# An attention kernel with a maxout behind it: output stores issued by ScalarE, and batch sums of v taken by halves of the heads

## The chip, the cores and the metric

The kernel runs on one core of a Trainium2 chip. A core has five engines that work beside each other, each through its own list of instructions in a fixed order: TensorE (PE) for matmuls, VectorE (DVE), ScalarE (ACT) and GpSimd (POOL) for elementwise work, and SyncE (SP), which here only issues transfers (DMAs). Engines wait for each other through semaphores. The metric is the time of one execution in microseconds (us) on the device, as a median of several runs.

## The reference

The inputs are q, k and v of 4 batches, 8 heads, 768 positions and 64 features, and three weight matrices. Cut to what matters:

```python
k_sum = k.reshape(B, H, nb, block, D).max(axis=3)       # block = 32, nb = 24
v_sum = v.reshape(B, H, nb, block, D).mean(axis=3)
scores_l = scale * np.matmul(q, k.transpose(0, 1, 3, 2)) # kept where |i - j| < 16
scores_s = scale * np.einsum('bhsd,bhnd->bhsn', q, k_sum) + np.log(block)
a = softmax(np.concatenate([masked scores_l, scores_s], axis=-1))
attn = np.matmul(a, np.concatenate([v, v_sum], axis=2))
x = attn.transpose(0, 2, 1, 3).reshape(B * S, H * D)    # 3072 x 512
g = np.maximum(x @ w1, x @ w2)                           # 3072 x 1024
out = g @ w_out                                          # 3072 x 512, float32
```

Each position attends to its near neighbours and to 24 block summaries, the largest k and the mean v of each block of 32. The attention's output goes through a maxout and a last matrix.

## The kernel before, in words

The work is written as a list of operations, each with an engine, an estimated time, what it reads and writes, and a priority. A planner (`Plan`, L112 to L188) goes through time in steps of 0.02 us and gives each engine the first operation in order of priority whose inputs are ready and whose buffers are free. What comes out is a fixed order of instructions per engine; the planner's times have no further part in the execution. `bump` in `CFG` shifts the priority of single operations.

For each batch and pair of heads, k and q are loaded (L361, L366), cast to bf16 and turned so that features lie on partitions: by PE (L509) or, for some pairs of the later batches, by transposing DMAs that SP issues (L471, L476). The scores of 64 positions at a time are matmuls with 64 rows of contraction (L566), ACT takes the exponential (L591), DVE masks (L598), and PE multiplies with v (`values`, L614), whose 64 x 65 blocks are written in pairs to the upper and the lower 64 rows. DVE divides by the sum (L627), and the result is turned by PE or by a DMA (L632) into `xt`.

The v side is `cast_v` and `spread_v`. A tile `vx` holds for each 64 positions a 128-row operand: rows of v, and in 32 of its rows the block means, the same for every one of the six 128-position groups. `spread_v` copies the odd groups (L407), lets PE sum the blocks with a matrix `amean` (L421), evicts the sums from PSUM to a tile `sums` (L434) and copies that into the rows of `vx` that want it (L438 to L443). For batch 0 this runs per pair of heads, for batches 1 to 3 once for all eight heads. For batches 1 and 2 the last copies are DVE's, for batch 3 they are two DMAs issued by SP (L448).

The maxout works on 256 positions at a time: four matmul groups with w1 − w2 (L723) with a ReLU on ACT behind each (L728), and then for each half of 128 positions the output (`out_part`): matmuls with w2's product (L744) and with g (L751), a copy from PSUM to a tile `o` (L754, four such tiles in turn), mostly by ACT, and a store to DRAM (L762). Rows are shifted by 16 positions, so that the last block of a batch wraps and needs a second, short store (L764). The very last block is cut into three column parts; the store of its first part is issued by ACT, those of the others, copied by DVE, by SP. All other stores are issued by SP, in SP's fixed order among loads and transposing DMAs.

The helper `copy` (L451) records a copy on DVE, ACT or POOL, so most copies have the line L456 in the profile.

The program was built for both kernels, and each DMA in it signals its landing on one of eight semaphores, taken in turn in the order of the program; before a DMA is issued, its engine waits until the DMA that used the same semaphore eight places earlier has landed.

Of the kernel before, what the change touches and what calls it, by code (L numbers as in the profile page):

```python
# [16 lines left out]
ACT = mybir.ActivationFunctionType  # L17

CFG = dict(
    kd="....D..DD.DD", xd="D...DD.DD.DDDDDDDD", tus=(1.6, 1.0, 1.2), kc="ADDA", qc="APPP", kp="DADD", qp="DDDA",
    tl="AADA", od="DADP", se="DADA", sr="DPdP", vc="ADPA", sc=4, s0=4, ph=1, ph0=2, av=4, lkp="DDDA", lxt="DADAAD",
    idle=40, pz=1, wd="PPDD", w1b="DPFD", w1t="AAAA", wo="PAAD", xt="DDDDDA", kv=(0.2, 1.2, 4.2, 4.2), sp=0.7,
# [56 lines left out]
class Task:  # L81
    done, start = 1e9, None
# [29 lines left out]
class Plan:  # L112
# [9 lines left out]
    def op(self, engine, us, fn, read=(), write=(), change=(), touch=(), behind=(), prio=0.0, label="", port=False):  # L122
        t = Task()
        t.engine, t.us, t.fn, t.label = engine, us, fn, label
        t.port = engine == "POOL" or port and engine == "DVE"
        t.prio = (prio + CFG["bump"].get(label, 0), len(self.tasks))
        t.new, t.behind = [*write, *change], behind
        t.deps = {w for b in (*read, *change) for w in b.writers}
        for b in t.new:
            b.writers.append(t)  # L130
        for b in (*read, *touch, *t.new):
            b.users.append(t)
        self.tasks.append(t)
        return t
# [57 lines left out]
def kernel(  # L192
# [14 lines left out]
    nc = tc.nc  # L207
    B, H, S, D = 4, 8, 768, 64
# [6 lines left out]
    NM, J, VW = S // 128, S // 128, 66  # L215
# [3 lines left out]
    op = plan.op  # L219
# [157 lines left out]
    def by_parity(b):  # L377
        return vx[b].ap[:].rearrange("p (m w) h c -> p w m h c", w=2)
# [12 lines left out]
    def spread_v(b, h0, h1, prio, engines):  # L391

        n, hs = h1 - h0, slice(h0, h1)
        src = [mains[b, hp] for hp in range(h0 // 2, h1 // 2)]
        out = [vx[b], *(ready[b, hp] for hp in range(h0 // 2, h1 // 2))]
        took, ps, st = Buf(Ring([None])), Buf(banks, "mm"), Buf(stg)
        tag, whole = f"{b}{h0}", n == H
        s_rows = slice(96, 128)
        if whole:
            fresh = Buf(Ring([None]))  # L400
            op("POOL", 0.2, lambda: nc.gpsimd.memset(by_parity(b)[s_rows, 0, :, :, D:VW], 1.0),
               read=[mains[b, 0]], write=[vx[b], fresh], prio=prio, label=f"ones {b}")
            src = [*src, fresh]

        def odd(lo, hi, ms, shift):
            w, ds = by_parity(b), slice(0, VW if whole else D)
            return (w[lo:hi, 1, ms, hs, ds],  # L407
                    w[lo:hi, 0, slice((ms.start + shift) % NM, (ms.stop + shift - 1) % NM + 1), hs, ds])

        for i, (lo, hi, ms, shift) in enumerate((  # L410
                (64, 128, slice(0, NM), 0), (0, 32, slice(0, NM - 1), 1), (0, 32, slice(NM - 1, NM), 1))):
            cols = (ms.stop - ms.start) * n * D
            move(engines[0], {"D": 0.12 + cols * 0.0003, "P": 0.06 + cols * 0.00095, "A": 0.2 + cols * 0.00083,
                              "S": (2.0, 0.83, 0.2)[i]},
                 lambda lo=lo, hi=hi, ms=ms, shift=shift: odd(lo, hi, ms, shift),
                 read=src, write=[*out, took], prio=prio, label=f"odd v{tag}{i}")

        def sums():
            w = by_parity(b)
            for m in range(NM):  # L420
                nc.tensor.matmul(out=bank(ps, n * D), lhsT=amean[:, m, :], rhs=w[:, 0, m, hs, 0:D],  # L421
                                 start=(m == 0), stop=(m == NM - 1))
# [22 lines left out]
    def move(engine, us, aps, label, **kw):  # L445
        if engine != "S":
            return copy(engine, us, aps, label, **kw)
        op("SP", us["S"], lambda: (lambda o, i: nc.sync.dma_start(  # L448
            out=o.rearrange("p m h c -> p m (h c)"), in_=i.rearrange("p m h c -> p m (h c)")))(*aps()), label=label, **kw)

    def copy(engine, us, aps, label, port=True, **kw):  # L451
        engine = ENG[engine]
        us = us if isinstance(us, float) else us[engine[0]]
        def fn():
            o, i = aps()
            {"DVE": nc.vector.tensor_copy, "ACT": nc.scalar.copy,  # L456
             "POOL": nc.gpsimd.tensor_copy}[engine](out=o, in_=i)
        op(engine, us, fn, label=label, port=port, **kw)

    def on(e):  # L460
# [277 lines left out]
    def out_part(b, grp, u, x, g, o, c0, c1, prio, engine, on_act):  # L738
        ps, cols, part = Buf(banks, "mm"), slice(c0, c1), (c1 - c0) / 512
        sl, done = slice(128 * u, 128 * u + 128), Buf(Ring([None]))  # L740

        def first():
            for c in range(KC):
                nc.tensor.matmul(out=bank(ps, c1 - c0), lhsT=x.ap[:, c, sl], rhs=w1o[c].ap[:, cols],  # L744
                                 start=(c == 0), stop=False)

        op("PE", 0.87 * part, first, read=[x, *w1o], write=[ps], prio=prio + 1, label=f"out {b}{grp}{u}")
        for n in range(2):
            def more(n=n):
                for f in range(4 * n, 4 * n + 4):  # L750
                    nc.tensor.matmul(out=bank(ps, c1 - c0), lhsT=g.ap[:, f, sl],  # L751
                                     rhs=wo[f // 2].ap[:, f % 2, cols], start=False, stop=(f == FC - 1))
            op("PE", 0.87 * part, more, read=[g, *wo], change=[ps], prio=prio + 1, label=f"out {b}{grp}{u}")
        copy(engine, {"A": 0.18 + 0.42 * part, "D": 0.15 + 0.55 * part}, lambda: (  # L754
            o.ap[:, cols], bank(ps, c1 - c0)),
             read=[ps], write=[o, done], prio=-1, port=False, label=f"copy out {b}{grp}{u}")

        def store():
            at = grp * GT + u * 128 + 16
            n = min(128, S - at)  # L760
            queue = nc.scalar if on_act else nc.sync
            queue.dma_start(out=out[b * S + at:b * S + at + n, cols], in_=o.ap[0:n, cols])  # L762
            if n < 128:
                queue.dma_start(out=out[b * S:b * S + 128 - n, cols], in_=o.ap[n:128, cols])  # L764
# [92 lines left out]
```

## Time and profile before

| | |
|---|---|
| median of 3 runs | 173.17 us (172.45 to 174.05) |
| the profiled execution | 174.17 us, its span 172.5 us |
| PE busy | 160.5 us |
| DVE busy | 102.4 us |
| ACT busy | 93.9 us |
| POOL busy | 41.7 us |
| moved by DMA | 35.82 MB, mean 208 GB/s |
| granted TensorE clock | 1.0 throughout |

The page of the profile shows one execution: the busy time of each engine, the span in 40 slices with the busy share of each in tenths, the DMA queues, the chain of work that ended last (followed back from the last instruction, at each step to what released it), and the costliest groups of instructions. A name such as `ACT o L456` is an instruction of ACT at line 456 that writes tile `o`; `SPq` is an instruction of SP's queue that issues a DMA, and its duration includes what it waits for while it issues. The trace behind the page answers in rows of a timeline: start and duration in us, engine, line, operation, out<-in, count, and in brackets the idle time before it with what ended it. Instructions that are not an engine's own work, such as the issue of a DMA, are not counted as busy.

### The profile page before, as it was taken

What the parts mean: (1) busy time and instruction counts of PE and PEld (TensorE: products, weight loads), DVE (VectorE), ACT (ScalarE), POOL (GpSimd) and SP (SyncE); (2) the same over time, 40 slices, a digit from 0 to 9 for tenths busy, and PEclk for the clock granted to TensorE, in tenths of its full rate; (3) what the DMA queues carried; (4) which work ended last, traced back from release to release, by engine and by line L of the source; (5) the groups of instructions that cost most, each with busy time, mean ns of one, the idle gap of its engine ahead of it and who ended that gap; (6) DMA issues with size and microseconds to landing.
All of it is one profiled execution on the core that took longest, in us unless ns stands there. A gap on an engine that the chain in (4) does not pass through costs nothing.

```text
span 172.5 us, 4501 instructions
## 1 busy us (share of the span) xinstructions
PE 160.5 (93%) x1841; PEld 106.6 (62%) x1841; DVE 102.4 (59%) x220; ACT 93.9 (54%) x146; POOL 41.7 (24%) x73
## 2 busy tenths in 40 slices
PE   4785898999999999999999999999998899999992
PEld 4765566997564565585574665745746658756662
DVE  6788998997679995649946466636364560000001
ACT  3766873789752658172284583852763706524420
POOL 7715899042134250053101101100400100000000
PEclk9999999999999999999999999999999999999999
DMA  5999999999999999996597999795588726011113
GB/s 169 307 321 279 313 392 379 301 288 350 297 291 192 289 335 276 174 144 183 105 209 158 345 233 215 153 241 122 99 207 132 206 51 182 2 61 65 61 61 122
DMA packets 68980, 35.82 MB, mean 208 GB/s; under 512 B 56544, under 2 KB 62944, under 8 KB 68960
## 3 DMA queue, kind: packets, MB, share of 16 engines
q1 hardware_dynamic: 68816, 35.41, 82.8%
q8 instruction: 14, 0.23, 0.6%
q10 hardware_dynamic: 144, 0.13, 0.2%
q14 instruction: 6, 0.05, 0.1%
HBM read 25.17 MB, written 6.29 MB: 182 GB/s over the span
## 4 chain that ended last, share of the span: by engine, by line
PE 63%; DMA 17%; SPq 14%; DVE 2%; issue 1%; ACT 1%; POOL 0%; DVEq 0%
PE banks L723 20%; PE banks L751 19%; PE banks L744 8%; DMA wf<-in_moe_w_dram 6%; SPq L366 5%; PE banks L707 4%; PE banks L614 4%; DMA kqf<-in_q_dram 4%; DMA vf<-in_v_dram 3%; SPq L372 3%; PE banks L509 2%; PE banks L566 2%; DMA vx<-sums 2%; SPq L659 2%; PE banks L421 2%
## 5 line engine op out<-in xcount | busy, mean ns | idle before, releaser
L751 PE MATMUL banks<-wo,g 128*128 128x512 bf16 (+2 forms) x208 | 46.9, 363 | 0.0
L723 PE MATMUL banks<-xt,wd 128*128 128x256 bf16 x384 | 46.5, 273 | 0.0
L723 PEld LDWEIGHTS <-wd 128*128 128x128 bf16 x384 | 36.8, 98 | 6.6
L728 ACT ACTIVATE g<-banks 128x512 bf16<-128x512 f32 x48 | 28.6, 598 | 15.6 <-PE banks L723 15.5
L456 ACT COPY o<-banks 128x512 f32<-128x512 f32 (+1 forms) x24 | 13.8, 576 | 35.3 <-PE banks L751 21.2
L751 PEld LDWEIGHTS <-g 128*128 128x128 bf16 x208 | 18.5, 98 | 17.8
L744 PE MATMUL banks<-w1o,xt 128*128 128x512 bf16 (+2 forms) x104 | 23.7, 363 | 0.0
L456 POOL CAST kqb<-kqf 128x768 bf16<-128x768 f32 x12 | 11.2, 934 | 39.2 <-PE banks L509 16.6
L591 ACT ACTIVATE pba<-banks 128x1024 bf16<-128x1024 f32 x16 | 16.4, 1023 | 5.6 <-PE banks L566 5.6
L528 DVE TENSOR_REDUCE ks<-kx 128x24 bf16<-128x768 bf16 x16 | 15.0, 946 | 6.0 <-DMA kx<-kqb 5.8
L627 DVE TENSOR_TENSOR xs<-banks,inv 128x512 bf16<-128x512 f32 x24 | 16.3, 686 | 0.6
L456 DVE COPY o<-banks 128x128 f32<-128x128 f32 x2 | 0.6, 290 | 26.8 <-PE banks L751 26.8
L744 PEld LDWEIGHTS <-xt 128*128 128x128 bf16 x104 | 9.8, 98 | 8.8
L598 DVE TENSOR_TENSOR pba<-pba,mask 128x1024 bf16<-128x1024 bf16 x12 | 8.3, 688 | 7.9 <-ACT pba L591 7.9
L456 POOL CAST vx<-vf 128x768 bf16<-128x768 f32 x7 | 6.4, 917 | 25.0 <-DMA vf<-in_v_dram 24.9
L566 PEld LDWEIGHTS <-kx 64*128 64x128 bf16 x416 | 7.4, 96 | 7.5 <-issue 6.3
L456 ACT CAST kqb<-kqf 128x768 bf16<-128x768 f32 x9 | 7.9, 881 | 6.7 <-DMA kqf<-in_q_dram 2.7
L456 DVE CAST kqb<-kqf 128x768 bf16<-128x768 f32 x11 | 6.7, 637 | 6.2 <-DMA kqf<-in_k_dram 4.4
L456 POOL COPY kx<-kx 128x32 bf16<-128x32 bf16 (+1 forms) x12 | 4.9, 405 | 22.2 <-DMA kx<-kqb 16.0
L785 PE MATMUL banks<-zeros 128*128 128x128 bf16 x80 | 8.5, 259 | 1.8 <-DVE zeros L781 1.8
L566 PE MATMUL banks<-qx,kx 64*128 64x64 bf16 (+2 forms) x416 | 9.4, 190 | 0.5 <-issue 0.5
L591 ACT ACTIVATE pbb<-banks 128x512 bf16<-128x512 f32 x16 | 9.6, 598 | 0.2 <-PE banks L566 0.2
(82 smaller groups left out, 189.7 us busy)
## 6 DMA issues: line engine op xcount, KB each, us to landing
kqf<-in_k_dram SPq DMA_DIRECT2D x16, 384.0 KB, 6.2
kqf<-in_q_dram SPq DMA_DIRECT2D x16, 384.0 KB, 5.7
vf<-in_v_dram SPq DMA_DIRECT2D x16, 384.0 KB, 6.4
out_dram<-o SPq DMA_DIRECT2D x19, 256.0 KB, 3.8
wf<-in_moe_w_dram SPq DMA_DIRECT2D x4, 1024.0 KB, 9.4
wf<-in_moe_w_out_dram SPq DMA_DIRECT2D x2, 1024.0 KB, 8.9
out_dram<-o SPq DMA_DIRECT2D x4, 224.0 KB, 2.5
vx<-sums SPq DMA_DIRECT2D x2, 198.0 KB, 3.6
```

The costliest lines, as they stand in the source:

```text
L366: op("SP", (1.2, 1.13)[n], lambda f=f, src=src: nc.sync.dma_start(out=f.ap[:], in_=src[b, 2 * hp:2 * hp + 2].rearrange("h (p j) d -> p h ( ...
L456: {"DVE": nc.vector.tensor_copy, "ACT": nc.scalar.copy, "POOL": nc.gpsimd.tensor_copy}[engine](out=o, in_=i)
L528: op("DVE", 0.95, lambda: nc.vector.tensor_reduce(out=ks.ap[:], in_=free(kt(), 128, [256, NM], [192, 2], [32, 2], [1, 32]), axis=AX.X, op= ...
L566: nc.tensor.matmul(out=bank(ps[i], 1024)[:, 512 * a + at + n0:512 * a + at + n1], lhsT=kx[b, hp].ap[r, 128 * t + 128:128 * t + 256], rhs=q ...
L591: op("ACT", (1.03, 0.6)[i], lambda: nc.scalar.activation(out=pv(), in_=bank(ps, 1024).rearrange("p (a c) -> p a c", a=2)[:, :, 0:64 * n], ...
L598: op("DVE", (0.69, 0.43)[i], lambda: nc.vector.tensor_tensor(out=pv(), in0=pv(), in1=m, op=ALU.mult), read=[mask_in], change=[pb], prio=pr ...
L627: op("DVE", 0.69, lambda: nc.vector.tensor_tensor(out=x.ap[:], in0=av()[:, :, :, 0:D], in1=inv.ap[:].to_broadcast([128, 2, 4, D]), op=ALU. ...
L723: nc.tensor.matmul(out=bank(ps)[:, 256 * s:256 * s + 256], lhsT=wd[n].ap[:, c, 128 * s:128 * s + 128], rhs=x.ap[:, c, :], start=(c == 0), ...
L728: op("ACT", 0.6, lambda n=n, ps=ps: nc.scalar.activation(out=g.ap[:, 2 * n:2 * n + 2, :].rearrange("p f n -> p (f n)"), in_=bank(ps), func ...
L744: nc.tensor.matmul(out=bank(ps, c1 - c0), lhsT=x.ap[:, c, sl], rhs=w1o[c].ap[:, cols], start=(c == 0), stop=False)
L751: nc.tensor.matmul(out=bank(ps, c1 - c0), lhsT=g.ap[:, f, sl], rhs=wo[f // 2].ap[:, f % 2, cols], start=False, stop=(f == FC - 1))
L785: nc.tensor.matmul(out=bank(ps, 128), lhsT=zeros[:], rhs=zeros[:], start=True, stop=True)
```

## The change

It has two parts.

First, where ACT copies an output block to its tile `o`, the store is no longer an operation of SP with a place in SP's order: ACT issues it itself, directly behind its copy (`copied`, with the short second store of a wrapped block). The operation `store` stays in the planner's list, but does nothing. The two stores behind DVE's copies stay with SP, and the one that ACT had issued stays with ACT. The planner sees the same operations with the same times, and so each engine's order is unchanged but for the stores themselves.

Second, the sums of v for batches 1 to 3 are taken by halves of the heads. In place of six matmuls of all 128 columns of `amean` with the 512 columns of eight heads, there are twelve in pairs: columns 0 to 63 of `amean` with heads 0 to 3 (256 columns) into PSUM rows 0 to 63, and columns 64 to 127 with heads 4 to 7 into rows 64 to 127 of the same 256 columns. Both halves of `amean` hold the same sums, so each half of the rows now has the sums of four heads. The eviction reads 256 columns instead of 512. The copies into `vx` are four of half the width instead of two, since the two groups of heads lie on different rows; for batch 3 that is four DMAs issued by SP.

```diff
+    smc="CCC",
...
+        halves = whole and CFG["smc"][b - 1] == "C"
+
         def sums():
             w = by_parity(b)
+            if halves:
+                for m in range(NM):
+                    for i in range(2):
+                        r = slice(64 * i, 64 * i + 64)
+                        nc.tensor.matmul(out=bank(ps, n * D // 2)[r], lhsT=amean[:, m, r],
+                                         rhs=w[:, 0, m, n // 2 * i:n // 2 * i + n // 2, 0:D],
+                                         start=(m == 0), stop=(m == NM - 1))
+                return
...
+        if halves:
+            sums_by_halves(b, ps, st, took, out, prio, engines)
+            return
...
+    def sums_by_halves(b, ps, st, took, out, prio, engines):
+
+        n = H // 2
+        copy(engines[1], {"D": 0.12 + H * D * 0.0011, "A": 0.18 + H * D * 0.00083}, lambda: (
+            st.ap[:, 0:n, 0:D], bank(ps, n * D).rearrange("p (h d) -> p h d", d=D)),
+             read=[ps, blocks_in], write=[st], prio=prio, port=False, label=f"sums {b}0")
+        cols = 6 * H * VW
+        for w, r in ((0, slice(96, 128)), (1, slice(32, 64))):
+            def aps(half, w=w, r=r):
+                frm = slice(32 + 64 * half, 64 + 64 * half)
+                return (by_parity(b)[r, w, :, n * half:n * half + n],
+                        st.ap[frm, 0:n].rearrange("p h d -> p (h d)").rearrange(
+                            "p (o h d) -> p o h d", o=1, d=VW).to_broadcast([32, NM, n, VW]))
+            move(engines[2], {"D": 0.12 + cols * 0.0003, "P": 0.06 + cols * 0.00095, "A": 0.2 + cols * 0.00083, "S": 1.0},
+                 aps, halves=True, read=[st, *([took] if w == 0 else [])], write=out, prio=prio, label=f"all sums {b}0{w}")
...
-        copy(engine, {"A": 0.18 + 0.42 * part, "D": 0.15 + 0.55 * part}, lambda: (
-            o.ap[:, cols], bank(ps, c1 - c0)),
-             read=[ps], write=[o, done], prio=-1, port=False, label=f"copy out {b}{grp}{u}")
-
-        def store():
+        own = engine == "A" and not on_act
+
+        def aps():
+            return o.ap[:, cols], bank(ps, c1 - c0)
+
+        def copied():
+            nc.scalar.copy(out=aps()[0], in_=aps()[1])
+            store(nc.scalar)
+
+        if own:
+            op("ACT", 0.18 + 0.42 * part, copied, read=[ps], write=[o, done], prio=-1, label=f"copy out {b}{grp}{u}")
+        else:
+            copy(engine, {"A": 0.18 + 0.42 * part, "D": 0.15 + 0.55 * part}, aps,
+                 read=[ps], write=[o, done], prio=-1, port=False, label=f"copy out {b}{grp}{u}")
+
+        def store(queue):
             at = grp * GT + u * 128 + 16
             n = min(128, S - at)
-            queue = nc.scalar if on_act else nc.sync
             queue.dma_start(out=out[b * S + at:b * S + at + n, cols], in_=o.ap[0:n, cols])
...
-        op("ACT" if on_act else "SP", 0.75 * part, store, read=[done], touch=[o], prio=-1, label=f"store {b}{grp}{u}")
+        queue = nc.scalar if on_act else nc.sync
+        op("ACT" if on_act else "SP", 0.75 * part, (lambda: None) if own else lambda: store(queue), read=[done], touch=[o], prio=-1, label=f"store {b}{grp}{u}")
```

`move` and `copy` take a new argument `halves`, with which one operation issues two instructions, one for each half.

More of the change, by code (lines that the diff above doesn't have):

```diff
@@ L443, in spread_v, with move, fn, copy @@
                  read=[st, *([took] if w == 0 else [])], write=out, prio=prio, label=f"all sums {tag}{w}")
-    def move(engine, us, aps, label, **kw):
-        if engine != "S":
[L447 to L451, printed above, removed]
+    def sums_by_halves(b, ps, st, took, out, prio, engines):
[12 more added lines that the diff above has]
+                 aps, halves=True, read=[st, *([took] if w == 0 else [])], write=out, prio=prio, label=f"all sums {b}0{w}")
+    def move(engine, us, aps, label, halves=False, **kw):
+        if engine != "S":
+            return copy(engine, us, aps, label, halves=halves, **kw)
+        def fn():
+            for o, i in [aps(0), aps(1)] if halves else [aps()]:
+                nc.sync.dma_start(out=o.rearrange("p m h c -> p m (h c)"), in_=i.rearrange("p m h c -> p m (h c)"))
+        op("SP", us["S"], fn, label=label, **kw)
+    def copy(engine, us, aps, label, port=True, halves=False, **kw):
         engine = ENG[engine]
@@ L454, in fn @@
         def fn():
-            o, i = aps()
-            {"DVE": nc.vector.tensor_copy, "ACT": nc.scalar.copy,
-             "POOL": nc.gpsimd.tensor_copy}[engine](out=o, in_=i)
+            for o, i in [aps(0), aps(1)] if halves else [aps()]:
+                {"DVE": nc.vector.tensor_copy, "ACT": nc.scalar.copy,
+                 "POOL": nc.gpsimd.tensor_copy}[engine](out=o, in_=i)
         op(engine, us, fn, label=label, port=port, **kw)
```

## The prediction

> **What bounds the kernel now.** I read the page's first parts, then the chain that ended last, then the timelines of TensorE (PE), of SyncE's queue (SP) and of ScalarE (ACT) over the stretches that the chain names. Page:
>
> ```profile
> PE 160.5 (93%) x1841; PEld 106.6 (62%) x1841; DVE 102.4 (59%) x220; ACT 93.9 (54%) x146; POOL 41.7 (24%) x73
> DMA  5999999999999999996597999795588726011113
> PE 63%; DMA 17%; SPq 14%; DVE 2%; issue 1%; ACT 1%; POOL 0%; DVEq 0%
> ```
>
> PE is busy nearly throughout, and ACT only half the time. The chain leaves PE for 31% of the span, in DMA and in SP's queue. At first that is the loading of the inputs, long before the first store; later it comes in short pieces. They show on PE's timeline (start and duration in us) as its only idle time behind the loading:
>
> ```profile
> 93.49 0.32 PE L614 MATMUL banks<-vx,pba 128*64 128x65 bf16 x8
> 94.17 0.57 PE L614 MATMUL banks<-vx,pba 128*64 128x65 bf16 x24 [0.36 <-DVE pba L598]
> 114.88 1.03 PE L751 MATMUL banks<-wo,g 128*128 128x512 bf16 x4
> 116.32 1.46 PE L421 MATMUL banks<-vx,amean 128*128 128x512 bf16 x6 [0.41 <-DVE vx L456]
> 129.24 0.22 PE L614 MATMUL banks<-vx,pba 128*64 128x65 bf16 x1
> 130.12 0.67 PE L614 MATMUL banks<-vx,pba 128*64 128x65 bf16 x31 [0.66 <-DMA vx<-sums]
> 132.94 1.92 PE L723 MATMUL banks<-xt,wd 128*128 128x256 bf16 x16
> 135.34 0.53 PE L566 MATMUL banks<-qx,kx 64*128 64x64 bf16 x26 [0.48 <-issue]
> ```
>
> The idle time in brackets, 1.91 us in all, leaves out the modelled tail of the matmul before, which PE normally overlaps with the next one. PE's pace comes from the chain, where each group stands with the time until the next:
>
> ```profile
> 55.32 1.29 PE banks L421 x6
> 69.29 0.63 PE banks L614 x32
> 69.92 1.83 PE banks L751 x8
> 143.24 5.24 PE banks L723 x48
> ```
>
> A 512-column matmul takes 1.29/6 = 0.215 us, a 256-column one 5.24/48 = 0.109, one of L614 0.63/32 = 0.02. So the four stalls cost 94.17 − (93.49 + 8 × 0.02) = 0.52, 116.32 − (114.88 + 4 × 0.215) = 0.58, 130.12 − 129.26 = 0.86, and 135.34 − (132.94 + 16 × 0.109) − 0.1 for a change of tile shape = 0.55: **2.5 us**. The trace names VectorE (DVE) twice, a DMA once and nothing once, yet the chain in front of the first stall shows who was late, and ACT's timeline when the data of those stores was ready:
>
> ```profile
> 77.90 0.52 SPq L762
> 78.47 0.42 SPq L762
> 78.95 0.44 SPq L764
> 86.64 6.29 DMA kqf<-in_q_dram
> 92.95 0.56 DVE kqb L456
> 93.51 0.61 DVE pba L598
> ```
>
> ```profile
> 74.26 0.58 ACT L456 COPY o<-banks 128x512 f32<-128x512 f32 x1 [0.28 <-PE banks L751]
> 85.56 0.58 ACT L456 COPY o<-banks 128x512 f32<-128x512 f32 x1 [0.28 <-PE banks L751]
> ```
>
> DVE stood in order behind a cast whose load was issued at 86.64, and that load stood in SP's queue behind three store issues of 1.49 us together, from 77.90 to 79.39. Those stores did not wait for their copies, the later of which was done at 74.84; they were served three microseconds late because SP issues back to back. Its queue is the limit, not the data. The store of the copy at 85.56 waited even until 92.29. The same holds further on (SP's timeline):
>
> ```profile
> 92.29 0.88 SPq L762 DMA_DIRECT2D out_dram<-o  x2
> 99.45 1.69 SPq L762 DMA_DIRECT2D out_dram<-o  x1
> 105.22 0.53 SPq L762 DMA_DIRECT2D out_dram<-o  x1
> 108.97 0.70 SPq L361 DMA_DIRECT2D kqf<-in_q_dram  x1
> 109.71 1.71 SPq L372 DMA_DIRECT2D vf<-in_v_dram  x1
> 111.51 1.68 SPq L762 DMA_DIRECT2D out_dram<-o  x1
> 126.41 0.60 SPq L448 DMA_DIRECT2D vx<-sums  x1
> L762 SPq DMA_DIRECT2D out_dram<-o x25: 332/526/3482, 57.5 to 169.7; - x25
> ```
>
> Stall two follows the v load issued at 109.71, stall three the second sums transfer of 126.41, stall four, by its place, the transposes queued behind that transfer. The instruction lists of the two kernels differ only in the moved and the split instructions, so each engine's order is otherwise as here.
>
> **Part one: the stores.** 23 of the 25 stores of L762 and the four short ones of L764 leave SP. Before stall one SP gets at least the 1.49 us back. Needed to remove it: its own 0.52 and what PE gains until then from part two (0.86, below), 1.38. That just suffices; the stores before 72 us help less, since the DMA digits are 9 until slice 18 (78 us), where the engines drain no faster, and 6 and 5 only behind it. Before stall two another 0.88 + 1.69 + 0.53 = 3.1 come on top: 4.6 against 0.58 + 1.38 = 2.0 needed. Before stall three 1.68 more, and three issues at the median of 0.53 (two of a wrapped block, one between the two sums transfers): 7.9, less 1.2 for two further sums issues (0.60 each), against 3.3 needed. Stall four has about the same lead. So I count all four as gone, −2.5. What is late next is PE itself, which follows its own order.
>
> What it adds is on ACT. The only ACT issue in this trace, and the places where ACT has the least room:
>
> ```profile
> 85.00:90.00 5.00, 5.00 (x64) 3.88 (x62) 3.13 (x9) 4.31 (x8) 0.51 (x1) 1.00 0.88 180
> 109.00 0.59 ACT L456 COPY o<-banks 128x512 f32<-128x512 f32 x1 [0.25 <-ACT xt L456]
> 109.48 0.81 ACT L456 COPY qx<-banks 128x768 bf16<-128x768 bf16 x1
> 111.81 0.53 PE L566 MATMUL banks<-qx,kx 64*128 64x64 bf16 x26
> 169.13 0.39 ACTq L762 DMA_DIRECT2D out_dram<-o  x1
> ```
>
> An issue took 0.39 on ACT, and on SP between 0.33 and 3.48, median 0.53. I take 0.45, next to the ACT row: SP's long ones come while loads of many small pieces fill its own queue, and ACT's holds stores alone. With the overlap of 0.1 that two ACT instructions otherwise have (0.59 long, 0.48 apart), a store costs ACT 0.55 and all 27 some 15 us, beside 78 us in which ACT is idle. What counts is the tightest place. Behind the copy at 109.00 two stores now run (the last block wraps), and behind them ACT has the qx copy, four ReLUs and two exps. The qx copy then ends at 109.59 + 2 × 0.5 + 0.81 = 111.4; PE's scores want it at 111.81. That holds up to 0.7 us an issue; from there PE pays twice the excess. From 85 to 90 us ACT is busy 4.31 of 5 (the fourth pair of figures in the row of the windows), and two stores fall inside: 5.4, so that this work may end 0.4 later, which the idle time behind each ReLU should take up. So 0 for ACT; bounds 0 and, at one issue of 3.48 in a tight place, +2.8.
>
> Stores now start up to 7 us earlier and may slow loads in flight. Between nothing and the full time of a store, 3.8 us from issue to landing by the median below, I take nothing: at stall one, where the lead is short, it would give back at most that stall and the gains before it (1.38); the later leads are larger.
>
> **Part two: the sums.** Six 512-column matmuls become twelve of 256 columns in pairs, each writing 64 of the 128 output rows. The kernel has that shape already: L614 writes 64 rows in pairs. 32 of these at 65 columns took 0.63; one after the other they would take 32 × 65/512 × 0.215 = 0.87, side by side 0.44. So pairs do run together, and 0.19 is left for the change of shape; the row behind it agrees (1.83 for eight against 8 × 0.215 = 1.72, 0.11 of it). New: 6 × 0.109 + 0.2 = 0.86 against 1.29, a gain of 0.43; three batches **−1.3**. Bounds: not side by side 12 × 0.109 + 0.2 = 1.51, +0.2 each; without any cost of the change −0.64 each.
>
> TensorEngine Tiling (Array Packing) in the Trainium skill speaks against the shape: under Restrictions, column tiling switches the fast weight load off, and under Key Properties a change of mode drains TensorE. The drain agrees with the 0.1 to 0.2 us above; slower weight loads would have to show in L614's 0.63 us for 32 loads and matmuls, so by that rule nothing is to be added here.
>
> The copies behind it, and the median landings used here and below:
>
> ```profile
> L456 DVE COPY vx<-sums 32x3168 bf16<-32x3168 bf16 x4 | 3.9, 978 | 0.1
> L456 DVE COPY vx<-vx 32x528 bf16<-32x528 bf16 x3 | 0.8, 270 | 0.0
> kqf<-in_q_dram SPq DMA_DIRECT2D x16, 384.0 KB, 5.7
> out_dram<-o SPq DMA_DIRECT2D x19, 256.0 KB, 3.8
> ```
>
> Two copies of 978 ns become four of 270 + 1056 × 0.268 = 553: +0.26 us on DVE. The eviction in front of them has half the columns and gets shorter by something of that size; I count the two as even.
>
> **Sum.** −2.5 − 1.3 = −3.8 us. The profiled execution took 174.17 us (span 172.5), 1.0 above the median of 173.17. 174.17 − 3.8 = 170.4 for it; carried to the median, **169.4 us**. More than 2.5 + 3 × 0.64 = 4.4 cannot go.
>
> **Rivals.**
> 1. *The loads land no earlier* (0.15). The transfers are the limit, not SP: for it, the DMA digits of 9 up to slice 18 and again in slices 23 to 25; against it, the 6 and 5 between. Then each stall ends when it does now and swallows the sums' gain before it, and nothing is gained: 173.2. Part of the leads would give 171 to 173; I put it at 172. DMA: Bandwidth & Descriptors in the Trainium skill has this under "Issuing engines are not separate DMA queues": another issuing engine saves only the sequencer's time. In this trace it is that time which is short at 77.90; by the rule as it stands the result would be near the 172.
> 2. *Pairs do not overlap* at 256 columns (0.07): the sums cost 0.2 more each instead of 0.43 less, −2.5 + 0.6 = −1.9, 171.3. Against it L614's 0.63.
> 3. *ACT stands still behind a store* (0.14), the slower case. Each DMA of this program signals one of eight semaphores in turn, and its issue waits until the DMA eight places earlier has landed. On SP those are loads and stores of its own; now ACT waits for loads of SP's. The worst is the short store behind 109.00's copy: its turn is that of the q load issued at 108.97, which by the median of 5.7 lands near 114.7. If SP had no lead, ACT would stop there for 5 us with the qx copy behind it, and PE's scores would start at 114.7 + 0.8 = 115.5 instead of 111.81, +3.7; the stalls that follow, 2.0 together, and the last batch's sums take part of it back. Some +2.4: 175.6. It decides once SP's lead there falls below about 3 us; I count 4.6. Issues on ACT of over 1.3 us would end in the same place.
>
> **How the numbers follow.** Forecast 0.64 (168.5 to 170.9), rivals 0.15, 0.07, 0.14. The range from 168.4 (all of 4.4, and some tenths of spread as the runs show) to 172.6 takes in the forecast, rival two and more than half of rival one, 0.8. About 1% is what a measurement of this kernel can tell from no change: faster by more, below 171.4, is the forecast, half of rival two and a little of rival one, 0.70; within 1%, 0.17; slower, rival three but for its mild end, 0.13.
>
> **What would show it.** Right: 28 ACT issues of 0.35 to 0.55; the load that landed at 92.93 landing before 91.5; no idle time over 0.3 on PE between 57 and 160; twelve matmuls of the sums in 0.65 to 0.7 us, and the next group 0.1 longer; PE's end near 165.3. Wrong: ACT idle with a store as the reason, most of all behind the short store of the wrapped block; PE waiting for qx or g; stalls at the old times in spite of an SP that is ahead.

## The result and the profile after

The changed kernel took **171.2 us** (median of 17 runs, 170.21 to 172.63), the kernel before, run beside it, 172.99 us (17 runs, 171.82 to 174.9). The ratio is 0.9911 (95% interval 0.9886 to 0.9935): 1.5 us faster, where 3.8 were forecast. Two later comparisons of the same two kernels gave 0.994 (0.9899 to 0.9981) and 0.9952 (0.9914 to 0.999). Ratios leave out runs of more than 1.5% above the fastest of their kernel; medians are over all runs.

The profiled execution took 172.63 us, the slowest of its 17, with a span of 170.9. From its page: busy times, two of the DMA queues (packets, MB, share of the engines), and the chain that ended last.

```profile
PE 159.0 (93%) x1859; PEld 106.5 (62%) x1859; DVE 105.7 (62%) x224; ACT 93.0 (54%) x146; POOL 42.2 (25%) x73
...
q1 hardware_dynamic: 65856, 29.38, 73.1%
q10 hardware_dynamic: 3520, 6.16, 10.6%
...
PE 64%; DMA 13%; SPq 10%; DVE 8%; issue 2%; POOL 1%; DVEq 0%; POOLq 0%
```

PE has 1.5 us less busy time, as the narrower sums let expect, DVE 3.3 more. The bytes of the moved stores now stand under a queue of their own, q10. In the chain SP's queue and DMA are down from 31% to 23%, and DVE is up from 2% to 8%. PE's timeline shows the sums, the places of the old stalls and the only row behind the loading that still has a bracket (the changed kernel has other line numbers: L427 are the sums, L785 the output matmuls, L806 and L808 the stores):

```profile
56.08 1.03 PE L785 MATMUL banks<-wo,g 128*128 128x512 bf16 x4
57.03 0.85 PE L427 MATMUL banks<-vx,amean 128*64 128x256 bf16 x12
57.81 0.53 PE L600 MATMUL banks<-qx,kx 64*128 64x64 bf16 x26
65.98 0.40 PE L674 MATMUL banks<-identity,xs 128*128 128x128 bf16 x4 [0.37 <-DVE xs L661]
116.60 0.84 PE L427 MATMUL banks<-vx,amean 128*64 128x256 bf16 x12
166.43 1.27 PE L785 MATMUL banks<-wo,g 128*128 128x256 bf16 x16
```

The four stalls of the forecast are gone, and the sums take 0.78 us until the next group (57.03 to 57.81); the group in front of them lasts 0.09 more than its four matmuls (0.95 against 4 × 0.215). Yet the first sums begin at 57.03, and in the profiled execution of before they began at 55.16, although no instruction ahead of them differs between the kernels. So from the first sums to the last group of matmuls there are 109.40 us, against 168.05 − 55.16 = 112.89 before: 3.5 us less. The start took 1.9 us of that back. Two readings are possible. Either the start differs from execution to execution, and the stalls are not always as large as in the one that I read, so that I measured the gain on an unusual execution (theory T). Or the changed kernel starts later by itself (rival U).

### The profile page after: what moved, and what is told of

Same layout as the page of the kernel before. It is cut to its first block, busy times and chain, and to the rows that moved or that the text cites. A ratio compares the mean times of both kernels' runs of the same rounds, so it can differ in the third digit from the quotient of the medians.

```text
span 170.9 us, 4532 instructions
## 1 busy us (share of the span) xinstructions
PE 159.0 (93%) x1859; PEld 106.5 (62%) x1859; DVE 105.7 (62%) x224; ACT 93.0 (54%) x146; POOL 42.2 (25%) x73
## 4 chain that ended last, share of the span: by engine, by line
PE 64%; DMA 13%; SPq 10%; DVE 8%; issue 2%; POOL 1%; DVEq 0%; POOLq 0%
PE banks L785 22%; PE banks L757 19%; PE banks L778 10%; DMA wf<-in_moe_w_dram 8%; DMA wf<-in_moe_w_out_dram 5%; SPq L367 5%; PE banks L741 4%; PE banks L648 3%; SPq L373 3%; DVE vx L490 3%; PE banks L600 3%; SPq L693 3%; PE banks L543 1%; DVE ks L562 1%; DVE qx L490 1%
## 5 line engine op out<-in xcount | busy, mean ns | idle before, releaser
L785 PE MATMUL banks<-wo,g 128*128 128x512 bf16 (+2 forms) x208 | 46.9, 363 | 0.0
L762 ACT ACTIVATE g<-banks 128x512 bf16<-128x512 f32 x48 | 27.8, 602 | 13.7 <-PE banks L757 13.5
L794 ACT COPY o<-banks 128x512 f32<-128x512 f32 x23 | 13.5, 587 | 32.4 <-PE banks L785 30.8
L785 PEld LDWEIGHTS <-g 128*128 128x128 bf16 x208 | 18.4, 98 | 17.7 <-issue 0.2
L490 POOL COPY kx<-kx 128x32 bf16<-128x32 bf16 (+1 forms) x12 | 5.5, 462 | 18.3 <-DMA kx<-kqb 12.1
L490 DVE COPY vx<-vx 64x3168 bf16<-64x3168 bf16 (+5 forms) x15 | 9.3, 632 | 0.2
```

Source lines behind the costliest of these rows:

```text
L490: {"DVE": nc.vector.tensor_copy, "ACT": nc.scalar.copy, "POOL": nc.gpsimd.tensor_copy}[engine](out=o, in_=i)
L762: op("ACT", 0.6, lambda n=n, ps=ps: nc.scalar.activation(out=g.ap[:, 2 * n:2 * n + 2, :].rearrange("p f n -> p (f n)"), in_=bank(ps), func ...
L794: nc.scalar.copy(out=aps()[0], in_=aps()[1])
```

## The experiments

From the start of the last group to the end of the span it is 4.4 to 4.5 us in all profiles but that of the thin stores (4.0), and 1.7 to 2.0 more to the time. So a profile is summed up by two numbers: when the first sums begin, and the **way** from there to the start of the last group of matmuls.

| kernel | first sums | last group | way | median | ratio to before |
|---|---|---|---|---|---|
| before (of the prediction) | 55.16 | 168.05 | 112.89 | 172.99 | |
| before, second | 56.74 | 167.04 | 110.30 | 172.73 | |
| before, third | 55.42 | 167.92 | 112.50 | 172.79 | |
| before, fourth | 54.58 | 167.35 | 112.77 | 172.79 | |
| changed, first | 57.03 | 166.43 | 109.40 | 171.20 | 0.9911 |
| changed, second | 55.96 | 165.36 | 109.40 | 171.29 | 0.994 |
| changed, third | 55.67 | 165.06 | 109.39 | 171.35 | 0.9952 |
| stores alone, first | 55.31 | 165.60 | 110.29 | 172.20 | 1.0003 |
| stores alone, second | 55.33 | 165.63 | 110.30 | 172.18 | 0.9987 |
| sums alone | 56.15 | 168.38 | 112.23 | 173.54 | 1.0081 |
| sums alone, batches 1 and 2 | 54.84 | 166.07 | 111.23 | 173.13 | 1.0001 |
| changed, reduction later | 54.89 | 163.74 | 108.85 | 170.40 | 0.9881 |
| changed, small loads on SP | 55.66 | 168.00 | 112.34 | 174.13 | 1.0078 |
| sums alone, thin stores | 55.67 | 165.06 | 109.39 | 171.14 | 0.9943 |

The medians of before are those of the runs beside each profile. The intervals of the ratios are 0.003 to 0.005 either way.

**Both kernels again.** No edit.

> The changed kernel again, for a second profile. In its first one the first matmuls of the sums (57.03 us) began 1.8 us later than in the kernel before (55.16), ahead of every moved store, and from there on the changed kernel gained 3.4 us. Theory T: the loading at the start differs by 1 to 2 us from execution to execution in both kernels, and the four stalls of 2.5 us were large in the one execution that I read; then this profile's first sums may begin anywhere between 55 and 57, with an end that follows, and no idle time of TensorE over 0.3 us between 58 and 160 us. Rival U: the changed kernel starts later by itself; then its first sums begin at 56.5 to 57.5 again.

> The kernel before again, for a second profile. T: its first sums may begin anywhere between 55 and 57 us, and the four stalls come out at another size, 0.5 to 2.5 us in all, smaller where the start is later. U: the first sums begin at 54.9 to 55.5 again, and the stalls are 2.2 to 2.8 us again.

The second profile of before has none of the four stalls. Its page has the chain, its timeline the places where they were:

```profile
PE 82%; DMA 8%; SPq 5%; ACT 1%; DVE 1%; issue 0%; DVEq 0%
```

```profile
95.07 0.70 PE L614 MATMUL banks<-vx,pba 128*64 128x65 bf16 x32
116.70 1.46 PE L421 MATMUL banks<-vx,amean 128*128 128x512 bf16 x6
129.63 0.70 PE L614 MATMUL banks<-vx,pba 128*64 128x65 bf16 x32
134.32 0.53 PE L566 MATMUL banks<-qx,kx 64*128 64x64 bf16 x26
```

None of these rows has a bracket, so PE did not stand before them. 110.3 us is then the way of the kernel before where TensorE alone sets it; what is above that is stalls: 112.89 − 110.30 = 2.6 us in the execution that I predicted from. U falls as it was put: over all profiles of the table and of the late kernels below, the first sums begin at 54.6 to 56.7 us (mean 55.5, eight profiles) with the stores on SP and at 54.9 to 57.0 (mean 55.8, eight) with them on ACT. A difference of some tenths is within that spread and stays open.

**Each part alone.** The stores alone: `smc="..."`. The sums alone: `own = False`.

> The stores alone issued by ScalarE, the sums as before. By the prediction -2.5 us, ratio 0.9855. T: -0.3 to -1.2 us, ratio 0.993 to 0.998, because the stalls of a usual execution are smaller than in the one profiled. U: 0 to -0.7 us, with the first sums at 56.5 to 57.5 us in the profile, if it is the moved stores that make the start late. If ScalarE stands still behind its stores (third rival of the prediction): 0 to +2 us, with idle time on ScalarE that a store ends.

> The sums by halves alone, all stores as before. By the prediction -1.3 us where nothing swallows it, ratio 0.9925. If the stalls of the kernel before are pinned to when loads land: the gain of 0.43 us at the second and third sums is swallowed by a stall that grows by as much, the sums save 0.4 to 0.9 us, ratio 0.995 to 0.998. T: either of the two, and with the stores alone the two parts add up to -1.6 to -1.8 us. U, with the sums as the cause of the late start: 0 to -0.4 us, first sums at 56.5 to 57.5 us.

The stores alone have a way of 110.29, the stall-free one, and the first ratio of 1.0003. The sums alone have no gain at all: they are 0.8% slower, with a way 2.8 us above the 109.4 that the same sums have with the stores on ACT. PE's timeline shows the old stalls:

```profile
94.81 0.57 PE L648 MATMUL banks<-vx,pba 128*64 128x65 bf16 x24 [0.45 <-DVE pba L632]
129.98 0.67 PE L648 MATMUL banks<-vx,pba 128*64 128x65 bf16 x31 [0.29 <-DMA vx<-sums]
135.66 0.53 PE L600 MATMUL banks<-qx,kx 64*128 64x64 bf16 x26 [0.94 <-DMA qx<-kqb]
```

So the parts do not add up: a PE that is ahead of the loads waits longer for them, and the sums alone bring nothing. The 2.8 us are those of the slowest of twelve executions (174.86 us, the median is 173.54), so the stalls of a usual one may be smaller.

**Sums alone without the two additional transfers.** `smc="CC."` and `own = False`.

> Sums by halves in batches 1 and 2 alone, batch 3 with two transfers as before, all stores issued by SyncE. The sums by halves alone in all three batches were 0.8% slower than the kernel before. If the two additional transfers that SyncE issues for batch 3 (1.2 us) are the cause: now 0 to -0.8 us against the kernel before, ratio 0.995 to 1.000, the stall near 135 us not over 0.6 us. If the cause is that TensorE comes earlier and so every stall behind the loads grows: 0 to +1 us, ratio 1.000 to 1.006, with stalls at 94 and 116 us larger than 0.5.

The ratio is 1.0001 (0.9958 to 1.0045), between the two expectations. PE's only wait of over 0.3 us behind 64 us is now for batch 3's sums, and the stall that was at 135 us is down to 0.24 us, at 133:

```profile
128.37 0.67 PE L648 MATMUL banks<-vx,pba 128*64 128x65 bf16 x31 [0.42 <-DMA vx<-sums]
```

By these ratios the two transfers make up most of the 0.8%, though the two intervals just touch; the rest of the gain is still swallowed (a stall-free way would be 109.4 + 0.5 = 109.9, measured 111.23).

**What SyncE was short of.** The prediction held its issuing time for the limit. One kernel puts small issues back on SP, the other leaves all issues there (`own = False`) and takes most of the bytes away (8 of 128 rows are stored, the other rows of the output are left out; the short stores likewise).

```diff
+        def small():
...
+            for _ in range(2 if S - at < 128 else 1):
+                t = const.tile([1, 16], F32, name=f"small{len(smalls)}")
+                smalls.append(t)
+                nc.sync.dma_start(out=t[:], in_=q[0, 0, 0:1, 0:16])
...
-        op("ACT" if on_act else "SP", 0.75 * part, (lambda: None) if own else lambda: store(queue), read=[done], touch=[o], prio=-1, label=f"store {b}{grp}{u}")
+        op("ACT" if on_act else "SP", 0.75 * part, small if own else lambda: store(queue), read=[done], touch=[o], prio=-1, label=f"store {b}{grp}{u}")
```

```diff
-            queue.dma_start(out=out[b * S + at:b * S + at + n, cols], in_=o.ap[0:n, cols])
+            queue.dma_start(out=out[b * S + at:b * S + at + 8, cols], in_=o.ap[0:8, cols])
```

> The changed kernel, with a load of 64 bytes issued by SyncE at each place in its order where a store stood (27 in all): SyncE's time is taken as before, the stores themselves stay with ScalarE. T (it is SyncE's time that makes loads late): issues of 0.3 to 0.5 us each, SyncE 1.5 to 4 us later than in the changed kernel at 104 us, stalls of TensorE of 0 to 2 us in all, from the first sums to the last group 109.4 to 111.4 us, time 0 to 2 us above the changed kernel's, and more spread. Rival (it is the bytes of the stores in SyncE's queue, 256 KB each, that hold its later issues up): SyncE no more than 1 us later, no stall, 109.4 us and the time of the changed kernel.

> The sums by halves alone, all stores issued by SyncE as in the kernel before, but each store writes only 8 of its 128 rows (the other rows of the output are left out): the same number of issues and the same order, a sixteenth of the bytes. The full version took 173.5 us, the changed kernel 171.3. T (the issuing by SyncE is what makes its loads late): 173 to 174 us, with stalls of 1 us and more. Rival (the bytes of the stores, in SyncE's queue among its loads, make them late): 171 to 172 us and no stall.

The thin stores speak against my theory as I put it. There are as many issues in the same order on SP, and yet the way is 109.39 us, that of the changed kernel, and the time is 171.14 us against 173.54 with whole stores. The same load of k is issued 6.5 us earlier than in the profile with whole stores (the first sums 0.5); SP's timeline with whole stores, then with thin ones:

```profile
64.34 3.50 SPq L806 DMA_DIRECT2D out_dram<-o  x1
105.71 0.53 SPq L806 DMA_DIRECT2D out_dram<-o  x1
107.62 0.57 SPq L362 DMA_DIRECT2D kqf<-in_k_dram  x1
```

```profile
63.16 1.79 SPq L806 DMA_DIRECT2D out_dram<-o  x1
98.99 0.42 SPq L806 DMA_DIRECT2D out_dram<-o  x1
101.10 0.58 SPq L362 DMA_DIRECT2D kqf<-in_k_dram  x1
```

Where nothing seems to hold it up, an issue costs 0.53 with the bytes and 0.42 without; the medians of these stores are 0.53 and 0.32. So the thin issues are also shorter by 0.1 to 0.2 us each. For the eleven ahead of that load this is 1 to 2 us of the 6, an estimate; the rest came back with every issue still in place. The 6.5 are from two single profiles. Over all profiles that load is issued at 101.6 to 103.9 us in the seven with the stores on ACT (the small loads below left out), and at 104.0 to 108.3 in the seven with whole stores on SP, on average 3.8 later. DMA: Bandwidth & Descriptors in the Trainium skill ("Issuing engines are not separate DMA queues") lets another issuing engine save the sequencer's issue time alone; here nearly all of the issue time stayed with SP in the thin kernel, and the stalls went all the same. In the changed kernel the page of the profile counts the stores under q10 instead of q1.

The small loads are the other half of the test: SP has 27 issues again, while the bytes of the stores stay in ACT's queue. SP's timeline, then that of the changed kernel's third profile, whose first sums began at the same time (55.66 and 55.67 us):

```profile
64.37 2.45 SPq L816 DMA_DIRECT2D small<-in_q_dram  x1
73.48 3.06 SPq L510 DMA_TRANSPOSE kx<-kqb  x2
104.76 0.58 SPq L362 DMA_DIRECT2D kqf<-in_k_dram  x1
```

```profile
70.27 3.92 SPq L510 DMA_TRANSPOSE kx<-kqb  x2
101.93 0.57 SPq L362 DMA_DIRECT2D kqf<-in_k_dram  x1
```

SP is 3.2 us late at 73 us and 2.8 at the load of k, as I had expected of its issuing time, and an issue of 64 bytes took up to 2.45 us (the thin store at that place 1.79, the whole one 3.50). So its own bytes are not all that makes an issue long. The two kernels together show that both count: with the issues kept and the bytes gone SP is ahead, and with the issues kept and the bytes moved by ACT's queue part of its lead is lost. How the two share, and whether an issue waits for its own queue to drain, for transfers of both queues or for one of the eight semaphores, stays open.

The small loads were also to bring stalls back, and did so (way 112.34), but PE waited for no load: the cause is the **third rival** of the prediction. ACT's and PE's timelines, and two rows of the chain between them:

```profile
109.74 0.58 ACT L795 COPY o<-banks 128x512 f32<-128x512 f32 x1 [0.20 <-PE banks L786]
112.24 0.34 ACTq L807 DMA_DIRECT2D out_dram<-o  x1
112.89 0.37 ACTq L809 DMA_DIRECT2D out_dram<-o  x1
113.29 0.80 ACT L490 COPY qx<-banks 128x768 bf16<-128x768 bf16 x1 [2.96 <-DMA out_dram<-o]
```

```profile
114.14 0.53 PE L600 MATMUL banks<-qx,kx 64*128 64x64 bf16 x26 [1.48 <-ACT qx L490]
```

```profile
106.87 5.99 DMA out_dram<-o
112.89 0.37 ACTq L809
```

With 27 more DMAs the turn of the eight semaphores shifts, which is how I explain what follows; the trace names only the store that was waited for. At the wrapped block the long store's issue comes at 112.24, though its copy was done at 110.32, and by the chain the short one waits for a store that ACT issued at 106.87 and that lands 5.99 us later. ACT stands for 2.96 us with the qx copy behind it, and PE for 1.48. It is the place that the prediction named, though what lands late is a store of ACT's own and not a load of SP's, with less than the 3.7 us of its price. With another 0.82 and 0.45 us at 79 us, behind the short store of the wrapped block before, it takes 2.75 of the 2.94 us by which the way grew. SP's lateness thus cost PE nothing here.

**The 0.4 us of the way that the sums did not bring.** Three times 0.43 us were forecast; the way is shorter by 110.30 − 109.40 = 0.90. From the first sums to the second it is not shorter at all (78.80 − 55.96 = 22.84; second profile of before 79.55 − 56.74 = 22.81). DVE's and PE's timelines of the changed kernel's second profile, then DVE's of the second profile of before (`...` stands for rows left out):

```profile
58.30 3.01 DVE L490 COPY vx<-sums 32x1584 bf16<-32x1584 bf16 x4
62.48 0.94 DVE L562 TENSOR_REDUCE ks<-kx 128x24 bf16<-128x768 bf16 x1
...
63.56 1.29 DVE L661 TENSOR_TENSOR xs<-banks,inv 128x512 bf16<-128x512 f32 x2
```

```profile
64.91 0.40 PE L674 MATMUL banks<-identity,xs 128*128 128x128 bf16 x4 [0.37 <-DVE xs L661]
```

```profile
59.17 1.99 DVE L456 COPY vx<-sums 32x3168 bf16<-32x3168 bf16 x2
```

The four copies take 3.0 us where two took 2.0 (0.4 of this comes back in the two masks behind them, 1.65 and 1.21 us in these profiles), and PE waits 0.37 us for a product of DVE. This wait is new; no profile without the narrower sums has it. As a test, the 0.94 us reduction, which is not needed until later, goes behind the divisions:

```diff
+        late = next(t for t in order if t.label == "max k13")
+        order.remove(late)
+        order.insert(next(i for i, t in enumerate(order) if t.label == "sums k13"), late)
         for t in order:
             t.fn()
```

> The changed kernel once more, beside the three others of this call. T (its path from the first sums on is set by TensorE alone, only the start varies): from the start of the first sums (now between 55 and 57 us) to the start of the last group of matmuls it takes 109.4 us, as in its two profiles so far (57.03 to 166.43, 55.96 to 165.36), to within 0.1. Rival: that agreement is chance; then 109 to 111.

> The changed kernel with one operation of VectorE moved: the reduction of k's last pair of batch 1 (0.94 us) comes behind the two divisions that TensorE waits 0.37 us for at 65 us, instead of in front of them. T (VectorE swallows the gain of the first sums: the four copies take 3.0 us where the two of the kernel before took 2.0): the wait of 0.37 us goes, the way from the first sums to the last group of matmuls takes 109.0 instead of 109.4 us, and the time is 0.4 us below the changed kernel's. Rival (the wait is moved on to the next product of VectorE): 109.3 to 109.5 us, and the same time as the changed kernel.

The wait is gone, the way is 108.85, and the time is 170.40 us (six runs, 169.81 to 171.15), ratio 0.9881 (0.9834 to 0.9928) against 171.35 and 0.9952 of the changed kernel beside it. The way accounts for 0.55 of the 0.95 us; the rest is within the intervals. It is the fastest version of the study.

Why the copies are slow: one of the four took 1234 ns, the others 563 to 567. It is the last, at 60.1 us, and lies beside a cast of POOL's. The group of the four copies (shortest, median, longest, first and last start) and POOL's timeline in the same profile, then POOL's in the second profile of before:

```profile
L490 DVE COPY vx<-sums x4: 563/567/1234, 58.3 to 60.1; 32x1584 bf16<-32x1584 bf16 x4
```

```profile
60.06 0.82 POOL L490 CAST vx<-vf 128x768 bf16<-128x768 f32 x1
```

```profile
61.22 1.35 POOL L456 CAST vx<-vf 128x768 bf16<-128x768 f32 x1
```

In the kernel before the copies were over by then (59.17 + 1.99 = 61.16), and it was this cast that was slow, beside DVE's masks. That the two engines hinder each other there is read from these rows alone; no run tried it.

**How often the stalls are there.**

> The kernel before, a third profile. Its two so far: first sums at 55.16 us and 112.9 us from there to the last group of matmuls, with four stalls; first sums at 56.74 and 110.3 us, with none. T: the stalls are what changes from execution to execution, so the way lies anywhere from 110.3 to 113 us, and the longer, the later SyncE issues its loads (86.0 and 108.3 us for two loads of k in the profile with stalls, 84.4 and 104.2 in the one without). Rival: the profile with four stalls was a single odd one; then 110.3 to 110.6 us again.

> The kernel before, a fourth profile, with the same expectations: by T a way of 110.3 to 113 us that goes with SyncE's lateness, by the rival 110.3 to 110.6 us.

Two more profiles of before have stalls of 2.2 and 2.5 us. That is three of four; but then the stores alone, which have none, should have gained 2 us. Theory A holds to such stalls in most executions, theory B to an average of 0.5 us. To measure the stalls over executions that were only timed, seven more matmuls make PE late ahead of the first sums:

```diff
+            for _ in range(7 if whole and b == 1 else 0):
+                nc.tensor.matmul(out=bank(ps, n * D), lhsT=amean[:, 0, :], rhs=w[:, 0, 0, hs, 0:D],
+                                 start=True, stop=True)
             for m in range(NM):
```

> The kernel before with seven more 512-column matmuls of TensorE in front of the first sums (7 x 0.215 = 1.5 us of work whose result is not used), so that TensorE is late by 1.5 us against the loads. Theory A (stalls of 2.2 to 2.6 us are in most executions, as in three of four profiles, and end when loads land): they take up most of the 1.5 us, and the time rises by 0 to 0.5 us. Theory B (stalls average 0.5 us over the executions that were timed): the time rises by 1.0 to 1.5 us.

> The kernel with the stores alone on ScalarE, with the same seven matmuls. It has no stalls in its profile, so by both theories its time rises by 1.5 us, and TensorE's way from the start of the seven matmuls to the last group becomes 111.8 us (110.3 + 1.5).

> The kernel with the stores alone on ScalarE, without the seven matmuls, beside the two others. A: 1.5 to 2.5 us below the kernel before, ratio 0.986 to 0.991. B: 0.2 to 0.8 us below, ratio 0.995 to 0.999. The first such comparison gave 1.0003 (0.9965 to 1.004).

In the control, the stores alone, the time rose from 0.9987 to 1.007 of before, 1.4 us, and its profile shows the 1.5 in full (56.81 to 168.61, 111.80). The kernel before rose by only 0.48% (0.15% to 0.82%), 0.8 us, between what the two theories expected. So some 0.6 to 0.7 us of the additional work was hidden, good to about 0.6 us, and this is an estimate of the average stall (of a stall above 1.5 us only a part could be hidden). Two others are lower: the stores alone, without a stall in both profiles, gain 0 and 0.2 us by their ratios (0.5 by the medians), and the three ratios of the changed kernel, 1.5, 1.0 and 0.8 us, leave 0.6, 0.1 and −0.1 for the stalls when the 0.9 of the sums is taken off. All lie nearer to theory B than to A. The late kernel before has no stall in its profile, as the second profile of before, whose first sums came late by chance:

```profile
55.14 1.67 PE L421 MATMUL banks<-vx,amean 128*128 128x512 bf16 x7
56.65 1.46 PE L424 MATMUL banks<-vx,amean 128*128 128x512 bf16 x6
166.94 1.27 PE L754 MATMUL banks<-wo,g 128*128 128x256 bf16 x16
```

From 56.65 it is 110.29 us. Late by 1.5 us, PE has none of the 2.2 to 2.6 us of stalls that the three others show. In both stall-free profiles SP too was ahead of the others (its load of k that comes at 108.34 us in the prediction's profile came at 104.0 and 104.2). Why SP is ahead when the first sums come later was not tried and stays open, as does the share of executions that have stalls: four profiles cannot count it, and all four were slower than the medians beside them. Nor did any run try whether an execution that is profiled by itself differs from those that are only timed.

## Why the prediction was wrong

**The step that failed** is the term of the stalls: 2.5 us, taken from one execution and then carried to the median with the rest of −3.8. They were real there, all four went as forecast, and a profile of the changed kernel against that execution shows 3.5 us on the way. But over the timed executions they average between 0 and 0.7 us by the estimates above. The profiled execution was 1.0 us above the median, and I took that as a shift that applies to before and after alike, where most of it could be the very thing that the change removes. With 0 to 0.7 in place of 2.5, and 0.9 in place of 1.3, the sum is −0.9 to −1.6; the three ratios give −1.5, −1.0 and −0.8. Why three of four profiled executions had stalls so far above the average stays open.

**The sums**: the mechanism held (0.78 us and 0.09 in front of them; forecast 0.86 against 1.29), so the second rival is out. The term was 1.3 and is 0.9, because I counted DVE's copies as even with the shorter eviction. They cost 1.0 us more in batch 1, since one copy slowed to 1234 ns, and the first of the three gains ended in a wait for DVE. Nor could the eviction pay for them there: in batch 1 it runs on ACT (0.59 us, now 0.37), and DVE came to the copies from another copy of its own. In batch 2, where DVE evicts, it went from 0.67 to 0.41 and the copies from 2.18 to 2.52 (second profiles), about even as counted. "What is late next is PE itself" was wrong at that place.

**The stores**: SP's lead was there, on average 3.8 us at the load of k where I counted 4.6, but the prediction's working for it was wrong. I added up issue durations (1.49, 0.88, 1.69) as time that SP gets back. At a long issue much of it is not got back, since the next issue takes it over. At the same place before and with the stores alone, SP's timeline:

```profile
63.79 3.48 SPq L762 DMA_DIRECT2D out_dram<-o  x1
67.36 1.32 SPq L632 DMA_TRANSPOSE xt<-xs  x1
```

```profile
63.14 4.67 SPq L666 DMA_TRANSPOSE xt<-xs  x1
```

A store issue of 3.48 us was removed, the transpose behind it grew from 1.32 to 4.67, and it was done at 67.81 instead of 68.68: 0.9 us came back, not 3.5. What I had not counted at all is that the stores' bytes hold SP up: with most of them gone SP was ahead with all its issues, as the thin stores show.

**ACT** at no cost: right. Here are its issues (ns: shortest, median, longest) and one row of its timeline, all of the first profile after:

```profile
L806 ACTq DMA_DIRECT2D out_dram<-o x24: 338/340/433, 57.8 to 167.5; - x24
L808 ACTq DMA_DIRECT2D out_dram<-o x4: 447/526/989, 76.2 to 166.3; - x4
```

```profile
111.35 0.80 ACT L490 COPY qx<-banks 128x768 bf16<-128x768 bf16 x1 [1.04 <-PE banks L757]
```

The way with the stores alone on ACT, 110.29 us, is the stall-free 110.30 of before. The issue of a long store took 0.34 where I took 0.45; at the wrapped block the qx copy ended at 111.35 + 0.80 = 112.2, and PE did not wait for it. The third rival did not happen in the changed kernel, and it is real: the small loads showed it.

**The first rival** was put as "nothing is gained"; in its pure form it is out, since the loads are issued earlier on average and no profile with the stores on ACT has a stall that ends with a load. The sign that I had named against it does not tell: the cast that began at 92.95 when its load landed begins at 91.16 in the first profile after, but at 91.08 in the second profile of before too.

The rival's result, part of the leads at 172, was nearer than my forecast, by the average size of the stalls rather than by its reason. Of what was to be seen, "no idle time over 0.3" fails by the 0.37 us behind DVE alone, and PE's end near 165.3 came out at 166.3 to 167.7.

## What to carry over

A stall that depends on how two streams meet has a different size in each execution: before its length is put into a forecast, compare several profiles of the kernel before, and treat a profiled execution that is slower than the median as one that may have more of that stall. The duration of a long DMA issue is not its own price: where a store issue of 3.48 us went, the next issue grew by 3.35, so count on 0.3 to 0.5 us an issue and test the bytes by themselves. An instruction that is cut in two costs more in all (four copies of 0.57 us for two of 1.0, undisturbed), and one of the parts may come to lie beside another engine's work; look for who waits behind it.

## What the runs showed of the hardware

A load of k behind stores of 256 KB in SP's queue was issued at 104.0 to 108.3 us in seven profiles, at 101.6 to 103.9 in seven with these stores in ACT's queue, and at 101.1 in one with a sixteenth of their bytes in SP's. An issue of 64 bytes took up to 2.45 us in SP's queue, one of a 256 KB store 0.34 in ACT's. The way of TensorE, where it waits for no load, repeats to 0.01 us (109.40, 109.40, 109.39; 110.30, 110.29, 110.30), while its start differs by up to 2.5 us; so nearly all of the spread of such a kernel lies in its loading and in stalls. Pairs of matmuls with 64 output rows and 256 columns run side by side: twelve take 0.78 us, and 0.09 more in front of them, where six whole ones of 512 columns take 1.29.
